# Linear attention with a gated FFN on one core: reciprocals spread to the head rows by DMA, contractions padded to 128 rows, weights folded and read in another order

## The chip, the cores and the metric

The kernel runs on one core of a Trainium2 chip. The metric is the device time of one execution in microseconds (us). It is 310.28 us for the kernel before, the median of three runs between 310.15 and 311.46. One slow run of the kernel before took 315.74 us at a granted clock of 0.978, the six fast ones beside it 309.21 to 312.18 us at 0.988 to 1.0.

Engines are named as in the profile: PE is TensorE (PEld its weight loads), DVE is VectorE, ACT is ScalarE, POOL is GpSimd, and SP is SyncE, which issues most DMAs.

## The reference

One block of 2,048 tokens, width 640, 32 heads of 20 columns, then a gated FFN of width 1,536. All inputs are bfloat16.

```python
phi(y) = concat(softmax(y), softmax(-y))           # per head, 40 features
q, k, v = split(layernorm(x) @ wqkv)
pq, pk  = phi(q @ w_phi), phi(k @ w_phi)           # w_phi: one 20x20 matrix per head
kv, z   = pk^T v, sum_tokens(pk)                   # per head, over ALL tokens
h  = x + ((pq kv) / (pq z + 1e-6)) @ wo
h2 = h + ((layernorm(h) @ w_gate) * (layernorm(h) @ w_up)) @ w_down
```

Because `kv` sums over all tokens, the kernel has a KV stage (all sixteen 128-token tiles of k and v), then a transition (first numerators, first output projections), then an FFN stage into which the remaining q work is mixed.

## The kernel before: the parts that matter here

The kernel records its instructions as units and puts them into a fixed tuned order (a list `ORDER`). `cost`, `lat` and `dma` are only what the scheduler was told; they don't run on the chip.

The heads are cut into six chunks: five of six heads (120 rows) and one of two heads (40 rows). In a chunk's PSUM tile, rows 0 to 5 (or 0 and 1) hold the denominators and the numerators start at row 6 (`HG`). A reciprocal must be multiplied into the 20 rows of its head. Before, a small matmul with a 0/1 matrix `Em` copied each reciprocal to its 20 rows:

```python
def num_mm(b, c, pr):                      # contraction over kr = 120 or 80 rows
    mm(pr[0:m, 0:n], KV[0:kr, c, 0:m],      q[0:kr, c, :], True, False)
    mm(pr[0:m, 0:n], KV[0:kr, NG + c, 0:m], q[0:kr, NG + c, :], False, True)
    ...                                    # cut: the last chunk has one matmul

def expand(b, c, pr, m, em, rden):
    n = P * BLK[b][1]                      # 256 or 512 tokens
    mm(pr[0:m, 512:512 + n], em, rden, True, True)      # contraction over 6 or 2 rows
    rx = rx_p.new()
    ...                                    # cut: PSUM -> rx copy on ACT or DVE
    tt("vector", oT[b][0:m, n * c:n * (c + 1)], pr[0:m, 0:n], o, ALU.mult)

def num(b):
    for c in range(6):
        ...                                # num_mm, then
        act(lnd[0:nh, 0:n], pr[0:nh, 0:n], ACT.Ln)      # 1/d = exp(-ln d)
        act(rden[0:nh, 0:n], lnd[0:nh, 0:n], ACT.Exp, scale=-1.0)
        expand(b, c, pr, m, Em[0:nh, 0, 0:m], rden[0:nh, 0:n])

def watt(t):                               # output projection of one tile
    for c in range(6):
        m = HG + DH * (HG if c < NG else 2)             # 126 or 46 rows
        for (n0, n1) in ((0, 512), (512, D)):
            mm(pr[:, n0:n1], oT[b][0:m, ...], Wo6[0:m, c, n0:n1], c == 0, c == 5)
```

The softmax here doesn't subtract the row's maximum and nothing guards it: scores larger than these inputs give would overflow.

Of the kernel before, what the change touches and what calls it, by code (L numbers as in the profile page):

```python
# [495 lines left out]
6 0 16 7 1 11 12 24 2 17 19 13 30 43 49 39 45 51 5 8 3 14 27 10 4 15 18 9 29 32 21 25 22 34 37 42 56 58 61 66 69 73 47 52 36 40 44 48 38 46 50 53 20  # L496
23 26 28 31 33 35 41 71 77 64 70 68 74 59 65 55 62 57 63 72 54 60 67 75 79 82 86 98 85 89 95 106 87 101 109 121 139 142 198 218 78 88 92 80 84 91 94
100 103 108 111 110 117 76 83 81 90 96 115 126 131 199 221 123 135 119 124 132 145 185 193 223 224 97 102 105 93 99 107 113 116 125 128 134 129 138
112 120 104 114 118 133 140 153 230 227 149 144 127 160 154 173 184 169 175 147 155 189 196 177 187 141 148 136 146 152 161 201 208 232 228 122 170
179 183 157 168 182 194 200 204 206 219 207 211 192 202 130 137 143 150 176 180 249 275 181 191 151 158 164 214 234 239 292 303 159 197 205 174 195  # L500
213 215 217 229 235 241 240 254 156 166 163 172 178 188 210 222 333 307 278 291 250 261 265 272 284 288 334 308 162 237 257 262 226 260 264 269 273
279 282 286 283 294 236 243 242 252 258 268 295 300 335 331 267 276 259 270 277 287 313 317 381 389 244 251 297 255 263 281 299 304 312 316 321 315
328 293 311 271 280 289 323 338 340 384 393 374 375 377 379 380 399 400 403 404 406 414 416 318 327 309 322 325 339 348 352 385 397 419 356 363 324
332 349 344 351 359 391 398 421 336 343 342 347 337 354 360 371 395 401 422 362 368 346 353 355 365 370 390 409 408 423 165 186 171 301 310 248 314
190 167 290 245 274 306 326 364 345 369 203 212 216 220 231 238 247 253 266 209 225 233 246 256 298 319 329 341 412 415 410 413 427 429 430 433 434
437 441 378 387 382 392 426 402 425 432 436 443 450 463 445 442 444 449 466 464 469 474 448 447 457 461 453 452 458 462 470 468 472 477 478 479 483
489 494 504 508 510 517 518 525 530 505 514 520 524 538 536 543 546 285 296 302 305 320 330 358 418 439 350 357 361 366 372 373 388 405 420 471 482
486 484 488 496 481 490 493 500 487 491 495 497 503 501 506 507 499 498 502 519 529 531 535 537 512 511 516 522 547 561 572 576 582 580 590 593 539
549 571 573 578 585 592 596 367 376 383 386 394 396 407 438 455 411 417 424 428 435 440 451 459 475 431 446 454 460 465 480 526 533 544 456 467 473
476 485 492 509 515 527 581 599 601 597 604 605 554 560 564 559 563 568 575 583 587 619 623 624 567 577 586 591 600 602 613 617 618 562 570 574 584  # L510
595 598 627 632 633 631 638 640 644 647 635 645 654 661 667 670 676 680 607 611 612 675 684 686 603 608 609 622 626 629 610 614 615 625 628 630 634
636 637 663 668 669 674 679 682 687 692 694 700 704 707 643 646 648 653 656 658 639 641 642 649 651 652 681 685 688 695 697 699 709 716 724 727 732
733 741 747 719 728 736 738 755 743 748 754 729 737 742 745 750 751 760 769 715 721 726 731 739 758 762 764 521 550 553 557 558 579 589 594 606 513
523 528 532 540 542 551 556 565 534 541 545 548 552 555 566 569 588 766 774 775 777 780 782 787 789 793 616 620 621 683 690 693 666 672 677 740 749
752 659 664 671 722 730 734 735 753 757 761 767 696 702 759 768 772 807 813 814 797 801 802 794 798 799 800 804 805 803 806 810 812 816 817 847 850
855 858 862 865 824 827 830 833 836 838 808 809 811 818 821 823 831 835 840 848 852 854 829 832 837 841 844 846 849 853 857 859 863 867 869 874 876
877 880 881 885 891 868 870 871 872 875 887 893 904 878 886 890 892 896 897 915 917 873 879 882 883 888 901 905 916 650 655 657 660 662 665 673 678
691 706 710 712 713 717 718 723 725 744 689 698 701 703 705 708 711 714 720 746 756 763 765 770 771 776 778 786 790 795 796 815 820 822 773 781 783
819 825 828 779 784 788 785 791 792 842 851 856 860 864 866 889 899 903 908 826 834 839 843 845 861 894 902 910 913 924 928 929 933 937 938 936 941
943 918 922 923 940 946 947 927 931 932 884 895 900 907 911 914 958 962 964 967 969 972 898 906 912 939 942 944 948 952 954 957 960 966 968 971 974  # L520
979 982 983 973 977 980 984 986 987 996 1002 1004 1005 1008 1009 1016 1020 989 993 994 995 998 1013 1017 1021 1001 1007 1011 1012 1014 1018 1025 1030
992 997 999 1000 1003 1023 1028 1031 909 919 920 951 949 956 945 950 953 930 934 935 921 925 926 955 959 963 961 965 970 976 978 975 985 988 990 991
981 1015 1022 1029 1032 1006 1010 1019 1024 1027 1054 1058 1059 1033 1037 1038 1036 1040 1041 1045 1049 1050 1060 1064 1065 1066 1068 1069 1039 1043
1044 1057 1061 1062 1026 1034 1035 1051 1055 1056 1042 1046 1047 1048 1052 1053 1070 1073 1076 1080 1082 1067 1078 1081 1084 1085 1063 1072 1083 1086
1087 1071 1074 1075 1077 1079
# [10 lines left out]
def _build(ctx, nc, A_x, A_wqkv, A_w_phi, A_wo, B_w_gate, B_w_up, B_w_down, out):  # L536
# [19 lines left out]
    o0 = NT * 2 * D - 4 * NC * D - NC * 160  # L556
    Wnat, WT = [], []
    for w in range(2):
        Wnat.append(r1[:, o0:o0 + NC * D].rearrange("p (c n) -> p c n", c=NC))
        WT.append(r1[:, o0 + NC * D:o0 + 2 * NC * D].rearrange("p (a n) -> p a n", a=NC))  # L560
        o0 += 2 * NC * D
# [11 lines left out]
    rx_p = pool("rx", r2, 7168, 512, 2)  # L573
    ot_p = pool("ot", r2, 8192, D, 3)
# [22 lines left out]
    Em = view(sb("Em", 4 * P), "p (j n) -> p j n", j=4)  # L597
# [55 lines left out]
    def copy(eng, o, i):  # L653
        n = numel(o)
        if eng == "any":
            return R.add("vector", lambda e: e.tensor_copy(real(o), real(i)), [i], [o], cost=(n + 130) / 960.0,  # L656
                         alts=[("scalar", lambda e: e.activation(out=real(o), in_=real(i), func=ACT.Copy), 0.17 + n / 1200.0)])
        if eng == "scalar":
            return act(o, i, ACT.Copy)
        return R.add(eng, lambda e: e.tensor_copy(real(o), real(i)), [i], [o], cost=(numel(o) + 130) / 960.0)  # L660
# [10 lines left out]
    def load_x(t0, n):  # L671
        return dma(x_all[:, t0:t0 + n, :], A_x[0, P * t0:P * (t0 + n), :].rearrange("(t p) n -> p t n", p=P), n * 163840, reads=[], eng="scalar")
# [3 lines left out]

    load_x(0, 1)
    load_x(1, 1)
    R.add("scalar", lambda e: e.preload_act_table_set("natural_log_exp_and_others"), cost=1.3)
    dma(Wrows, A_w_phi.rearrange("h d f -> (h d) f").rearrange("(a p) f -> p a f", p=P), 25600, reads=[])  # L680
    load_w(Wnat[0], D)
    load_w(Wkv[:, :, D:2 * D], 2 * D)
    load_x(2, 2)
    load_x(4, 4)


    memset("gpsimd", Gm[:, :, :], 1.0)
    memset("gpsimd", ident[:, :], 0.0)
    afsel(ident[:, :], ALU.not_equal, 1.0, 0, [[-1, P]], 1)
    afsel(Gm[:, :, :], ALU.is_ge, 0.0, 0, [[P, NC], [-DH, H]], 1)  # L690
    afsel(Gm[:, :, :], ALU.is_ge, 0.0, DH - 1, [[-P, NC], [DH, H]], -1)
    for a in range(NC):
        lo, hi = CH[a]
        nh = hi - lo + 1
        tt("gpsimd", Phi[:, a, 0:nh, :], Wrows[:, a, :].unsqueeze(1).to_broadcast([P, nh, DH]),
           Gm[:, a, lo:hi + 1].unsqueeze(2).to_broadcast([P, nh, DH]), ALU.mult)
# [5 lines left out]
    memset("gpsimd", Zd[:, :, :], 1.0)  # L702
    memset("gpsimd", G6[:, :], 1.0)
    memset("gpsimd", Em[:, :, :], 1.0)
# [7 lines left out]
    afsel(Em[:, :, :], ALU.is_ge, 0.0, -HG, [[32 * DH, 4], [1, P]], -DH)  # L712
    afsel(Em[:, :, :], ALU.is_ge, 0.0, HG + DH - 1, [[-32 * DH, 4], [-1, P]], DH)
# [15 lines left out]
    def ln_apply(t, dst):  # L729
# [5 lines left out]
                                                         scalar2=mv[:, t, 3:4], op0=ALU.subtract, op1=ALU.mult), 0.7)])  # L735
# [3 lines left out]
    def fold_T(w, a):  # L739
        pb = psum.new(1)  # L740
        tb = pb.bitcast(BF16)
        with R.group():
            for a2 in range(NC):
                o, i = tb[:, P * a2:P * (a2 + 1)], Wnat[w][:, a2, P * a:P * (a + 1)]
                R.add("tensor", lambda e, o=o, i=i: e.transpose(out=real(o), in_=i, identity=ident[:, :]),  # L745
                      [i, ident[:, :]], [o], cost=0.1, lat=0.17)
        copy("any", WT[w][:, a, :], tb[:, 0:D])
# [271 lines left out]
    for a in range(NC):  # L1019
        fold_T(0, a)  # L1020
# [104 lines left out]
```

## Time and profile before

| | kernel before |
|---|---|
| time, median of 3 | 310.28 us |
| profiled execution (slow) | 316.35 us, span 314.6 us, mean granted clock 0.978 |
| PE busy | 298.4 us, 95% of the span |
| first denominator matmul (end of the KV stage) | 82.7 us |
| first gate/up matmul (start of the FFN stage) | 110.4 us, after 10.2 us at half clock |

These lines are from the summary page of the kernel before: the span, PE's busy time and share, PE's busy share and granted clock in 40 slices (a digit is tenths), and the chain of work that ended last, by engine.

```profile
span 314.6 us, 5099 instructions
...
PE 298.4 (95%) x2024; PEld 165.3 (53%) x2024; DVE 178.2 (57%) x321; ACT 158.2 (50%) x345; POOL 82.5 (26%) x58
...
PE   2899599999989999999999999999999999999995
...
PEclk9999899999957999999999999999999999999999
...
PE 77%; DMA 9%; POOL 6%; DVE 4%; ACT 1%; SPq 1%; issue 0%
```

PE is the limit: its row stands at 9 in nearly every slice, and 77% of the chain is PE. The 5 and 7 in the clock row are the 10.2 us at half clock. The timed runs of the same kernel had a granted clock of 0.994 to 1.0, so that stretch belongs to the slow profile and not to the 310 us.

The next lines are groups of matmuls of the kernel before, one line per shape. The columns are: line, engine, operation, output tile <- input tiles, rows*columns of the weights, rows x columns of the moving operand, count | busy us, mean ns of one | idle time before them.

```profile
L628 PE MATMUL ps<-wo,r 126*128 126x128 bf16 x80 | 17.8, 223 | 0.0
...
L628 PE MATMUL ps<-rden,Em 6*126 6x512 bf16 x15 | 6.4, 425 | 0.0
...
L628 PE MATMUL ps<-wo,r 46*128 46x128 bf16 x16 | 3.5, 216 | 0.0
L628 PE MATMUL ps<-rden,Em 6*126 6x256 bf16 x10 | 3.3, 378 | 0.0
```

These mean times are from start to modelled end, and neighbours overlap, so they can't be added. For a busy PE, the distance from one matmul's start to the next one's start is what counts, and I worked that out from the trace: 0.356 us for the 6-row, 512-column expansion, where a 128-row matmul of 512 columns takes 0.216; and 0.148 us for the 128-column matmul of the 46-row chunk, and about the same (0.152) for the 126-row one just before it, where others take 0.056.

### The profile page before, as it was taken

How to read it: one execution, taken by the hardware profiler on the slowest of the kernel's cores; microseconds unless marked ns; L12 is line 12 of the kernel's file. 1: busy time of each engine (PE TensorE's matmuls, PEld its weight loads, DVE VectorE, ACT ScalarE, POOL GpSimd, SP SyncE). 2: the span in 40 equal slices, each digit the busy share in tenths (PEclk: the TensorE clock that was granted, in tenths of full speed). 3: DMA queues.
4: the chain of work that ended last, by engine and by line, in shares of the span. 5: the costliest groups of instructions: out<-in, count | busy, mean ns of one | idle time of the engine just before them, and what ended most of it. 6: DMA issues, size and time to landing. Idle time of an engine off the chain costs nothing.

```text
span 314.6 us, 5099 instructions
## 1 busy us (share of the span) xinstructions
PE 298.4 (95%) x2024; PEld 165.3 (53%) x2024; DVE 178.2 (57%) x321; ACT 158.2 (50%) x345; POOL 82.5 (26%) x58
## 2 busy tenths in 40 slices
PE   2899599999989999999999999999999999999995
PEld 2555375657634588656465444445444444544453
DVE  4979669787846794365867324544434445423204
ACT  4779488866354854358276233638423443532200
POOL 6217854879931463003332300000000000000000
PEclk9999899999957999999999999999999999999999
DMA  7767929994960666002074500004100002300002
GB/s 237 206 96 163 234 69 189 217 190 136 260 133 2 133 70 113 2 21 58 11 141 78 93 0 2 22 23 85 42 2 0 0 21 65 83 2 0 0 2 83
DMA packets 58171, 25.84 MB, mean 82 GB/s; under 512 B 49279, under 2 KB 56867, under 8 KB 58147
## 3 DMA queue, kind: packets, MB, share of 16 engines
q1 hardware_dynamic: 56003, 22.89, 34.1%
q10 hardware_dynamic: 2144, 2.62, 3.0%
q8 instruction: 16, 0.26, 0.3%
q14 instruction: 8, 0.07, 0.1%
HBM read 11.05 MB, written 2.62 MB: 43 GB/s over the span
## 4 chain that ended last, share of the span: by engine, by line
PE 77%; DMA 9%; POOL 6%; DVE 4%; ACT 1%; SPq 1%; issue 0%
PE ps L628 77%; POOL r L645 4%; DMA r<-in_A_wqkv_dram 4%; DMA xnT<-xn 3%; DVE sr L768 2%; DMA pqT<-phq 2%; POOL phq L645 2%; PE ps L745 1%; SPq L622 1%; DVE sr L770 1%; ACT phq L639 0%; DVE st L718 0%; DVE xn L734 0%; DVE r L1003 0%; DVE wkv L656 0%
## 5 line engine op out<-in xcount | busy, mean ns | idle before, releaser
L628 PE MATMUL ps<-xnT,wgu 128*128 128x512 bf16 (+1 forms) x600 | 106.6, 337 | 0.0
L639 ACT ACTIVATE r<-ps 128x640 bf16<-128x640 f32 (+2 forms) x108 | 62.8, 595 | 73.8 <-PE ps L628 73.1
L645 DVE TENSOR_TENSOR r<-ps,r 128x512 bf16<-128x512 f32 (+5 forms) x90 | 51.5, 581 | 63.2 <-PE ps L628 51.8
L628 PEld LDWEIGHTS ps<-xnT,wgu 128*128 128x128 bf16 x600 | 57.8, 98 | 46.3 <-issue 1.7
L628 PE MATMUL ps<-r 128*128 128x512 bf16 (+5 forms) x620 | 72.8, 269 | 3.8 <-DMA r<-in_A_wqkv_dram 3.4
L628 PEld LDWEIGHTS ps<-r 128*128 128x128 bf16 (+2 forms) x620 | 44.0, 108 | 31.3 <-DMA r<-in_A_wqkv_dram 3.6
L645 POOL TENSOR_TENSOR phq<-phq,sr 128x1320 bf16<-128x1320 bf16 x16 | 38.7, 2424 | 63.3 <-DVE sr L806 61.3
L628 PE MATMUL ps<-wkv,xnT 128*128 128x512 bf16 x320 | 47.1, 305 | 2.0 <-DMA xnT<-xn 2.0
L645 POOL TENSOR_TENSOR r<-r,sr 128x1280 bf16<-128x1280 bf16 x16 | 37.5, 2362 | 27.1 <-DVE sr L770 23.8
L628 PEld LDWEIGHTS ps<-wkv,xnT 128*128 128x128 bf16 x320 | 24.9, 99 | 21.0 <-issue 3.4
L639 ACT ACTIVATE phq<-ps 128x600 bf16<-128x600 f32 (+1 forms) x64 | 24.7, 436 | 16.8 <-PE ps L628 14.7
L628 PE MATMUL ps<-wo,r 126*128 126x512 bf16 x192 | 30.8, 307 | 0.0
L1003 DVE SCALAR_TENSOR_TENSOR r<-ps,mv,x_all 128x640 bf16<-128x640 f32 x16 | 14.1, 883 | 23.8 <-PE ps L628 23.8
L628 PE MATMUL ps<-wq,xnT 128*128 128x512 bf16 (+1 forms) x160 | 25.3, 309 | 1.2 <-ACT lnd L639 1.2
L804 DVE TENSOR_REDUCE sr<-phq 128x66 f32<-128x1320 bf16 x16 | 24.2, 1512 | 3.0 <-ACT phq L639 2.2
L768 DVE TENSOR_REDUCE sr<-r 128x64 f32<-128x1280 bf16 x16 | 23.4, 1470 | 3.6 <-ACT r L639 2.2
L628 PEld LDWEIGHTS ps<-wo,r 126*128 126x128 bf16 x192 | 14.1, 99 | 15.5 <-issue 7.7
L964 DVE SCALAR_TENSOR_TENSOR x_all<-ps,x_all 128x640 bf16<-128x640 f32 x16 | 13.2, 823 | 11.7 <-PE ps L628 11.5
L628 PEld LDWEIGHTS ps<-wq,xnT 128*128 128x128 bf16 x160 | 12.5, 100 | 11.3 <-ACT lnd L639 1.6
L639 ACT ACTIVATE lnd<-ps 6x512 f32<-6x512 f32 (+3 forms) x22 | 11.9, 547 | 11.6 <-PE ps L628 11.3
L914 DVE CAST r<-ps 126x512 bf16<-126x512 f32 (+2 forms) x14 | 8.6, 615 | 15.4 <-PE ps L628 15.3
L968 ACT ACTIVATE xn<-x_all,mv 128x640 bf16<-128x640 bf16 x9 | 7.4, 827 | 17.3 <-DVE mv L650 17.3
(57 smaller groups left out, 171.2 us busy)
## 6 DMA issues: line engine op xcount, KB each, us to landing
out_dram<-r SPq DMA_DIRECT2D x16, 160.0 KB, 1.8
x_all<-in_A_x_dram ACTq DMA_DIRECT2D x3, 640.0 KB, 6.5
wgu<-in_B_w_up_dram SPq DMA_DIRECT2D x5, 384.0 KB, 3.9
wgu<-in_B_w_gate_dram SPq DMA_DIRECT2D x5, 384.0 KB, 4.3
r<-in_B_w_down_dram SPq DMA_DIRECT2D x6, 320.0 KB, 6.3
r<-in_A_wqkv_dram SPq DMA_DIRECT2D x1, 800.0 KB, 5.0
wkv<-in_A_wqkv_dram SPq DMA_DIRECT2D x1, 800.0 KB, 10.0
wo<-in_A_wo_dram SPq DMA_DIRECT2D x4, 157.5 KB
```

The lines of the kernel that those rows point to most:

```text
L622: return R.add("sync", lambda e: e.dma_start_transpose(real(dst), real(src)), rd, wr, cost=1.03 + 0.17 * nbytes / 163840, lat=1.0, dma=0.3 ...
L628: return R.add("tensor", lambda e: e.matmul(real(o), lhsT=real(l), rhs=real(r), start=start, stop=stop, **kw), [l, r], [o], cost=cost or m ...
L639: return e.activation(out=real(o), in_=real(i), func=func, scale=scale, **kw)
L645: return R.add(eng, lambda e: e.tensor_tensor(out=real(o), in0=real(a), in1=real(b), op=op), [a, b], [o], cost=cost)
L745: R.add("tensor", lambda e, o=o, i=i: e.transpose(out=real(o), in_=i, identity=ident[:, :]), [i, ident[:, :]], [o], cost=0.1, lat=0.17)
L768: R.add("vector", lambda e: e.tensor_reduce(out=real(sr)[:, 0:n], in_=real(v), axis=AX.X, op=ALU.add), [v], [sr[:, 0:n]], cost=0.13 + n * ...
L770: R.add("vector", lambda e: e.reciprocal(out=real(sr)[:, 66:66 + n], in_=real(sr)[:, 0:n]), [sr[:, 0:n]], [sr[:, 66:66 + n]], cost=0.56)
L804: R.add("vector", lambda e: e.tensor_reduce(out=real(r4(0)), in_=real(k4), axis=AX.X, op=ALU.add), [k4], [r4(0)], cost=0.13 + n * DH / 960.0)
L914: lat=0.08, alts=[("vector", lambda e: e.tensor_copy(real(o), real(i)), (n + 130) / 960)])
L964: R.add("vector", lambda e: e.scalar_tensor_tensor(out=h, in0=real(pr)[:, 0:D], scalar=1.0, in1=h, op0=ALU.mult, op1=ALU.add, accum_out=sm ...
L968: R.add("scalar", lambda e: e.activation(out=real(k), in_=h, func=ACT.Identity, bias=nm), [h, nm], [k], cost=0.83, lat=0.08, alts=[("vecto ...
L1003: R.add("vector", lambda e: e.scalar_tensor_tensor(out=real(k), in0=real(pr)[:, 0:D], scalar=r2, in1=h, op0=ALU.mult, op1=ALU.add), [pr[:, ...
```

## The change

The change does five things at once:

1. The `Em` matmul and its PSUM copy go. A DMA on SP's queue reads each of the 6 (or 2) rows of reciprocals and writes it to the 20 rows of its head in an SBUF buffer `rx` (four buffers).
2. The contractions of numerator and output projection are padded to 128 rows, so that PE has no row-count changes there. POOL clears `KV`, `rx` and the output weights `Wo6` for that, early.
3. Wk is loaded in five row pieces, and each piece is transposed as it lands.
4. The FFN's gate and up weights are read in the second half of the KV stage, x is loaded two tiles at a time, and some costs told to the scheduler were corrected.
5. The tuned order is a new one (the whole list of more than 1,000 numbers differs).

```diff
-    def expand(b, c, pr, m, em, rden):
-        n = P * BLK[b][1]
-        mm(pr[0:m, 512:512 + n], em, rden, True, True)
         rx = rx_p.new()
-        ...  PSUM -> rx copy on ACT or DVE
-        tt("vector", oT[b][0:m, n * c:n * (c + 1)], pr[0:m, 0:n], o, ALU.mult)
+        dst, o = rx[HG:HG + DH * nh, 0:n], oT[b][:, n * c:n * (c + 1)]
+        def spread(e):
+            v = real(rden)
+            (ps, k), inner = v.ap
+            return e.dma_start(real(dst), bass.AP(v.tensor, v.offset, [[ps, k], [0, DH], list(inner)]))
+        R.after(rx_clear, R.add("sync", spread, [rden], [dst], cost=0.45, lat=1.6, dma=0.25 + 0.0006 * n))
+        tt("vector", o, pr[:, 0:n], rx[:, 0:n], ALU.mult)
 ...
-                mm(pr[0:m, 0:n], KV[0:kr, c, 0:m], q[0:kr, c, :], True, False)
-                mm(pr[0:m, 0:n], KV[0:kr, NG + c, 0:m], q[0:kr, NG + c, :], False, True)
+                mm(pr[:, 0:n], KV[:, k, :], q[:, k, :], k == ks[0], k == ks[-1])
 ...
-                    mm(pr[:, n0:n1], oT[b][0:m, n * c + q:n * c + q + P], Wo6[0:m, c, n0:n1], c == 0, c == 5)
+                    mm(pr[:, n0:n1], oT[b][:, n * c + q:n * c + q + P], Wo6[:, c, n0:n1], c == 0, c == 5)
 ...
+    kv_clear = memset("gpsimd", KV[:, :, :], 0.0)
+    rx_clear = memset("gpsimd", rx_r[:, :], 0.0)
+    wo_clear = memset("gpsimd", Wo6[:, :, :], 0.0)
 ...
-    load_w(Wnat[0], D)                       # Wk in one 800 KB load
+    for i in range(1, NC):
+        first(load_k(i))                     # Wk in five row pieces
 ...
-            bulk(6 + 2 * c + g, Wgu[:, g, c, :], ...)     # behind KV tile 6 to 15
+            bulk(9 + c, Wgu[:, g, c, :], ...)             # behind KV tile 9 to 13
```

The expression `[[ps, k], [0, DH], ...]` is the spread's source: k rows (6 or 2), each read 20 times.

## The prediction

> **What bounds the kernel now.** TensorE. The summary has PE busy 95% of a 314.6 us span, DVE 57%, ACT 50%, POOL 26%; the chain of waits gives PE 77%, one unbroken piece from 88.1 to 311.4 us. Start-to-start times of neighbouring matmuls in the trace sum to 305 us; at their own best rate (0.216 us for 512 columns, 0.056 for 128) the same columns need about 278. The other 27 us are waits (first matmul at 5.96 us behind the 800 KB key-weight load; 3.4 us at 33 us for the transposed Wq; 0.4 to 1.6 us a few more times), half clock for 3.4 and 10.2 us, and matmuls that cost more than their columns. The profiled run is a slow one (316.4 us against 310.3); I take its 10.2 us at half clock to be most of that.
>
> **What the change removes.**
> 1. 30 reciprocal-expanding matmuls with 6 or 2 rows, 9.5 us of PE by start-to-start. A 6-row, 512-column one costs 0.356 us, not 0.216[...].
> 2. [...] its 128-column matmul takes 0.148 instead of 0.056, and so does the one ahead of it, 16 times each: 3 us. Around the numerator matmuls 1 to 1.5 us. Padding to 128 rows removes these and adds no columns.
> Both are on the critical path, as PE hardly waits after 88 us: 13 to 14 us.
> 3. 30 PSUM copies of the expanded reciprocals (13 us on ACT and DVE): off the path.
> 4. Front: Wk by row pieces starts the transposes about 2 us earlier, but all 25 still precede the folds. Gain about 2 us.
> 5. FFN weights later, x in two-tile loads, Wq transposes scheduled with a higher cost: the 3.4 us wait for Wq and the half clock after it mostly go: 2 to 4 us.
>
> **What it adds.** 30 spreading DMAs (about 0.45 us of issue each, from the plain DMAs' issue times). From denominator to scaled numerator the expand and copy (about 1.3 us) become an estimated 2.5 us (1.8 us landing of a 160 KB store in the DMA list, plus waiting behind transposes). In the FFN blocks other matmuls fill this. In the two small blocks between KV stage and FFN they do not: 18 numerator matmuls are followed directly by the output projection, with four spread buffers for twelve chunks, and ScalarE's Ln stands behind q exponentials that wait for transposes. I expect 2 to 4 us of PE idle there. POOL's 7 us of extra clearing (estimate from 0.53 us per 512 columns) falls where it idles, 10 to 22 us.
>
> **Sum.** 310.3 - 13.5 - 2 - 3 + 3 = about 295.0 us, range 289.0 to 302.0. Chances: faster 0.92, within 2% 0.06, slower 0.02.
>
> **What the profile should show.** No 6-row matmuls; the 128-column output-projection matmul at 0.056 throughout; PE busy down by about 13 us, ACT by about 8; first matmul at 3.5 to 4.5 us; no wait over 1.5 us for Wq; a new PE wait on DVE's products or the spreads near 85 to 95 us; PE unbroken in the FFN stage.
>
> **What would make it wrong.** Spreads that land later than 3 us and stall the output projection in every block (300 or more); a transition idle long enough to halve the clock for 10 us; or the old profile's half clock being in its timed runs too, and vanishing (288).

The extra time of matmuls at a change of row count was measured (0.356 us where a 128-row matmul takes 0.216, 0.148 where others take 0.056). Item 2 is about the 46-row chunk of the output projection.

## More of the kernel before

Busy time by stage (KV stage, transition, FFN stage) in the kernel before: stretch, its length, then busy time and instructions of each engine, granted clock, DMA share and GB/s.

```profile
0.00:82.70 82.70, 70.96 (x645) 45.99 (x649) 63.34 (x118) 57.50 (x110) 52.38 (x46) 0.98 0.77 182
82.70:110.40 27.70, 26.48 (x156) 12.27 (x154) 18.07 (x40) 16.20 (x48) 11.12 (x6) 0.82 0.57 100
110.40:314.60 204.20, 201.00 (x1231) 107.08 (x1229) 96.75 (x164) 84.49 (x188) 19.05 (x8) 1.00 0.19 39
```

In the FFN stage PE is busy for 201.0 of 204.2 us. The KV stage is the only one where it waits noticeably.

## The result

The changed kernel is correct and slower. Its median is 333.67 us (four runs, 333.06 to 335.6, all fast) against 310.79 us for the kernel before in the same rounds. The ratio is 1.0747, with a 95% interval from 1.0692 to 1.0801. A ratio here and below is the mean time of one kernel's fast runs over the mean of the other's fast runs of the same rounds, so it is not quite the ratio of the medians quoted beside it.

The same lines of the summary page, for the kernel after (a fast run):

```profile
span 333.7 us, 5044 instructions
...
PE 290.8 (87%) x1994; PEld 166.7 (50%) x1994; DVE 175.4 (53%) x309; ACT 149.5 (45%) x328; POOL 87.4 (26%) x58
...
PE   2798899898773886998899997999999959999995
...
PEclk9999799999795899799999998999999998999999
...
PE 51%; DMA 15%; DVE 14%; POOL 7%; SPq 6%; issue 4%; ACT 2%; DVEq 0%; ACTq 0%
```

PE lost about 8 us of busy time, as hoped, but the span grew by 19 us. The chain of waits, which was 77% PE, is now 51% PE and 15% DMA, 14% DVE. PE has holes (7, 7, 3, 5 in its row). The clock row drops around the longer ones: stretches at half clock follow the holes of 3.4, 2.1 and 2.7 us at 131, 204 and 272 us. Holes of 1.2 to 1.6 us at 117, 155 and 160 us have none behind them.

The same three stages in the kernel after. Its first denominator matmul starts at 91.6 us and its first gate/up matmul at 122.4 us.

```profile
0.00:91.60 91.60, 75.23 (x651) 49.28 (x651) 72.29 (x121) 58.37 (x112) 61.44 (x48) 0.96 0.71 175
91.60:122.40 30.80, 20.32 (x140) 10.16 (x138) 17.86 (x39) 12.73 (x40) 10.13 (x5) 0.83 0.64 92
122.40:333.70 211.30, 195.29 (x1209) 107.26 (x1207) 85.23 (x150) 78.37 (x180) 15.79 (x7) 0.97 0.25 45
```

All three stages are longer: by 8.9, 3.1 and 7.1 us. (Against a fast run of before the transition's difference is larger: 10.2 us at half clock in the profile before can cost up to 5.1, an estimate: a 512-column matmul takes 0.426 us from start to start at half clock there, 0.216 at full.) In the transition PE is idle for 10.5 of 30.8 us, in the FFN stage for 16.0 of 211.3.

The extra time is gone. These are the output projection's groups in the kernel after:

```profile
L626 PE MATMUL ps<-wo,r 128*128 128x512 bf16 x96 | 30.3, 412 | 6.9 <-DVE r L643 6.9
L626 PE MATMUL ps<-wo,r 128*128 128x128 bf16 x96 | 22.2, 231 | 2.7 <-DVE r L643 2.7
```

One shape is left, and its start-to-start time at the median is 0.056 us for 128 columns in the trace. But a new entry stands behind the last bar: 9.6 us of waiting for DVE's products, where before it said 0.0. What those products wait for is shown by everything that touches the buffer `rx` in the kernel after: the 30 spreads (their time is the issue on SP), the 30 products, what the products waited for, and who waited for the products.

```profile
L923 SPq DMA_DIRECT2D rx<-rden x30: 677/758/1740, 93.0 to 266.0; - x30
L643 DVE TENSOR_TENSOR r<-ps,rx x30: 415/691/693, 96.8 to 273.6; 128x512 bf16<-128x512 f32 x18, 128x256 bf16<-128x256 f32 x12
...
  DMA rx<-rden: 54.9, 25
...
  PEld ps L626: 21.1, 11
  PE ps L626: 17.4, 11
```

25 of 30 products had to wait for their spread, 54.9 us in all, and PE in its turn waited 17.4 us for products, 11 times. From the start of a spread's issue to the start of its product the trace gives 5.16 us at the median, 3.24 at the least, 7.60 at the most.

The longest one, in the last block, in the chain of waits of the kernel after (start, length, what):

```profile
254.84 8.67 PE ps L626 x49
...
265.02 0.61 ACT rden L637
265.64 0.32 ACT r L637
265.95 7.57 DMA rx<-rden
...
273.55 0.70 DVE r L643
274.25 0.05 issue
274.30 10.81 PE ps L626 x66
```

A spread of 7.6 us stands between ACT and DVE, and the chain comes back to PE only after it. PE had other work meanwhile, but one matmul starts at 271.25 us and the next one only 3.05 us later, 2.66 of it idle. Before, this part of the chain was inside one unbroken piece of PE, 223 us long:

```profile
88.11 223.30 PE ps L628 x1351
```

What one spread does was read from its packets. One that ran alone (issued at 240.79 us) shows 120 packets of 1,024 bytes and six small packets of 4 bytes. The first packet starts 1.43 us after the start of the issue and the last data packet ends at 4.74 us. The six small packets are completion writes. I take each for one DMA engine, so six engines: at most six of the 120 packets are in flight at once. In what was measured the number of these writes goes with the source's rows: two for the two-row spread issued at 260.06 us, six here, 12 in a_twelve (12 rows), 15 in a_wide (120 rows). The transfer took 3.3 us for 120 KB, 20 rows per engine. Two of the engines started a row every 0.08 us and had ended by 3.05 us after the start of the issue; the other four took about 0.17 us a row and ended the transfer.

The front did not gain. These are PE's first instructions in the kernel after:

```profile
4.00 0.69 PE L753 MATMUL ps<-ident,r 128*128 128x128 bf16 x5 [4.00 <-DMA r<-in_A_wqkv_dram]
7.28 2.31 PE L753 MATMUL ps<-ident,r 128*128 128x128 bf16 x20 [2.59 <-DMA r<-in_A_wqkv_dram]
```

Transposes begin at 4.0 us instead of 5.96, and then wait 2.6 us for the second Wk piece. The first projection of the KV stage starts at 12.2 us (12.3 before).

And on DVE the second layer norm of the front stands out (start, length, instruction), beside POOL's clearing of the output weights:

```profile
11.77 3.01 DVE L742 TENSOR_SCALAR xn<-x_all,mv 128x640 bf16<-128x640 bf16 x1
...
15.61 0.45 DVE L742 TENSOR_SCALAR xn<-x_all,mv 128x640 bf16<-128x640 bf16 x1
```

```profile
8.35 1.27 POOL L661 MEMSET KV<- 128x1408 bf16 x1
9.56 1.80 POOL L661 MEMSET rx<- 128x2048 bf16 x1
11.30 3.30 POOL L661 MEMSET wo<- 128x3840 bf16 x1
```

The same instruction takes 0.45 us at 15.6 us and 3.01 us at 11.8 us, ending just after POOL's memset (14.78 and 14.60 us). Not every DVE instruction beside a memset was slow: a copy from PSUM at 10.85 us took 0.82 us, as long as one at 15.97 us, after the memsets. That POOL held the layer norm off is my reading of the times; a_split and a_late test it. The second k/v projection starts at 17.4 us, 2.4 later than before.

### The profile page after: what moved, and what is told of

It reads as the page before. It is cut to its first block, busy times and chain, and to the rows that moved or that the text cites. A ratio compares the mean times of both kernels' runs of the same rounds, so it can differ in the third digit from the quotient of the medians.

```text
span 333.7 us, 5044 instructions
## 1 busy us (share of the span) xinstructions
PE 290.8 (87%) x1994; PEld 166.7 (50%) x1994; DVE 175.4 (53%) x309; ACT 149.5 (45%) x328; POOL 87.4 (26%) x58
## 4 chain that ended last, share of the span: by engine, by line
PE 51%; DMA 15%; DVE 14%; POOL 7%; SPq 6%; issue 4%; ACT 2%; DVEq 0%; ACTq 0%
PE ps L626 50%; DMA rx<-rden 12%; POOL r L643 6%; SPq L620 4%; DVE sr L778 4%; DVE sr L814 3%; SPq L923 2%; DMA r<-in_A_wqkv_dram 2%; POOL phq L643 1%; DVE r L643 1%; DMA x_all<-in_A_x_dram 1%; DVE sr L816 1%; DVE sr L780 1%; ACT r L637 1%; PE ps L753 1%
## 5 line engine op out<-in xcount | busy, mean ns | idle before, releaser
L626 PE MATMUL ps<-xnT,wgu 128*128 128x512 bf16 (+1 forms) x600 | 110.3, 341 | 3.4 <-DVE r L643 3.4
L626 PEld LDWEIGHTS ps<-xnT,wgu 128*128 128x128 bf16 x600 | 58.8, 99 | 51.3 <-DVE r L643 4.1
L637 ACT ACTIVATE r<-ps 128x512 bf16<-128x512 f32 (+2 forms) x92 | 52.0, 574 | 66.1 <-PE ps L626 60.4
L626 PE MATMUL ps<-r 128*128 128x512 bf16 (+5 forms) x620 | 74.3, 276 | 6.4 <-POOL r L643 3.2
L626 PEld LDWEIGHTS ps<-r 128*128 128x128 bf16 (+2 forms) x620 | 47.5, 113 | 32.4 <-POOL r L643 3.8
L643 DVE TENSOR_TENSOR r<-ps,r 128x512 bf16<-128x512 f32 (+1 forms) x60 | 34.1, 577 | 50.3 <-PE ps L626 43.4
L643 DVE TENSOR_TENSOR r<-ps,rx 128x512 bf16<-128x512 f32 (+1 forms) x30 | 17.4, 584 | 55.0 <-DMA rx<-rden 54.9
L626 PE MATMUL ps<-wo,r 128*128 128x512 bf16 x192 | 30.8, 321 | 9.6 <-DVE r L643 9.6
L626 PEld LDWEIGHTS ps<-wkv,xnT 128*128 128x128 bf16 x320 | 24.6, 98 | 22.1 <-DVE wkv L654 2.1
L626 PE MATMUL ps<-wq,xnT 128*128 128x512 bf16 (+1 forms) x160 | 26.3, 314 | 4.1 <-DVE r L643 4.1
L626 PEld LDWEIGHTS ps<-wo,r 128*128 128x128 bf16 x192 | 15.9, 105 | 23.7 <-DVE r L643 11.0
L976 ACT ACTIVATE xn<-x_all,mv 128x640 bf16<-128x640 bf16 x9 | 7.2, 825 | 27.3 <-DVE mv L648 25.3
```

The costliest lines, as they stand in the source:

```text
L626: return R.add("tensor", lambda e: e.matmul(real(o), lhsT=real(l), rhs=real(r), start=start, stop=stop, **kw), [l, r], [o], cost=cost or m ...
L637: return e.activation(out=real(o), in_=real(i), func=func, scale=scale, **kw)
L643: return R.add(eng, lambda e: e.tensor_tensor(out=real(o), in0=real(a), in1=real(b), op=op), [a, b], [o], cost=cost)
L976: R.add("scalar", lambda e: e.activation(out=real(k), in_=h, func=ACT.Identity, bias=nm), [h, nm], [k], cost=0.83, lat=0.08, alts=[("vecto ...
```

## The experiments

My theory after the result had two parts. **W**: the spreads take about twice the time that the order was made for, and that makes the transition and the FFN stage longer. **P**: POOL's early clearings hold DVE off and make the KV stage longer. Rivals were the new order as such, the traffic of the spreads on SP's queue, the later FFN weight loads, and the padding itself being worth less than thought.

Kernels named a_ are built from the kernel after, those named b_ from the kernel before. Four of the a_ kernels give a wrong result. The quoted expectations were written call by call; where one names theories by letters of its own, the words beside the letter count.

This table gathers the stage boundaries of the profiled runs; it is worked out from the first denominator matmul and the first gate/up matmul in each trace. "PE clock halved" lists the lengths of the stretches at half clock before the last matmul.

| kernel | KV stage | transition | FFN stage | PE clock halved, us | median us |
|---|---|---|---|---|---|
| before (slow run) | 82.7 | 27.7 | 204.2 | 3.4, 10.2 | 310.79 |
| after | 91.6 | 30.7 | 211.3 | 3.4, 3.4, 10.2, 3.4, 3.4, 3.4 | 333.67 |
| a_free | 89.2 | 31.1 | 192.4 | 10.2 | 315.20 |
| a_twelve | 92.7 | 24.9 | 194.0 | 3.4, 3.4, 3.4 | 311.75 |
| a_wide | 89.8 | 25.3 | 193.0 | 3.4, 6.8 | 310.26 |
| a_split | 92.6 | 30.4 | 210.9 | 3.4, 3.4, 10.2, 3.4, 3.4, 3.4 | 335.91 |
| a_late | 86.6 | 31.3 | 210.4 | 13.7, 3.4, 3.4 | 331.29 |
| a_latev | 88.7 | 30.0 | 211.5 | 3.4, 10.2, 3.4, 3.4, 3.4 | 331.53 |
| a_wlate | 87.2 | 24.6 | 193.0 | 3.4 | 306.65 |
| b_pad2 | 82.3 | 20.9 | 197.7 | 3.4 | 303.23 |
| b_padk2 | 82.3 | 22.5 | 200.6 | 3.4 | 306.77 |
| b_padw | 83.4 | 23.9 | 197.0 | 3.4, 3.4 | 307.81 |

The medians are over all runs; those of a_wlate and b_padw hold slow ones (306.25 and 306.40 without them). b_pad, a_expand, a_list and a_slow are left out and told below. Rows of the same order can be compared stage by stage: the eight from after to a_wlate, and the b_ rows with before. The two orders place the q work differently, so across them only the totals compare. The rows are single profiles, and they scatter: after, a_free, a_twelve and a_wide do nearly the same work up to the first spread, and yet their KV stages end between 89.2 and 92.7 us.

### a_free: nobody waits for a spread (wrong result)

The spreads write to a spare place, and the products read a constant. The order is that of the kernel after.

```diff
-        R.after(rx_clear, R.add("sync", spread, [rden], [dst], ...))
-        tt("vector", o, pr[:, 0:n], rx[:, 0:n], ALU.mult)
+        # scheduled as before, but written to a spare buffer and never read
+        u = R.add("sync", spread_to_spare, [rden], [dst], ...)
+        # the product reads rows of ones
+        u = R.add("vector", product_with_ones, ...)
```

> The kernel after, every instruction in the same order, but the spreads go to a spare buffer and the products read a constant, so nobody waits for a spread (wrong result on purpose). Theory L (latency of the spreads is what TensorE waits for after 92 us): the waits for products and spreads after 92 us, about 26 us, and most of the half clock after them go, 300 to 308 us. Rival K (the loss is in the KV stage and its new order): over 325 us. Either way the first denominator matmul stays at about 91 us.

Measured: 315.2 us median (four fast runs), ratio to before 1.0145, interval 1.0083 to 1.0206. The waits for spreads are gone, and the FFN stage falls from 211.3 to 192.4 us. The transition doesn't improve: spreads now go out without the products' throttle and pile up in the queue, a q transpose issued behind them holds PE for 9.7 us at 104.7 us, and 10.2 us at half clock follow. So the run says that the FFN stage's loss is the waits for spreads. For the transition it is spoilt by a wait of its own making. a_wide was the cleaner test.

### a_wide: the same waits, a copy that 15 engines carry (wrong result)

The spread copies 120 rows from a constant tile of 120 rows instead of 6 rows twenty times. It has the same bytes, the same issue and the same waits, and still waits for the reciprocals. POOL has one more memset early, for the constant.

```diff
-            return e.dma_start(real(dst), bass.AP(v.tensor, v.offset, [[ps, k], [0, DH], list(inner)]))
-        R.after(rx_clear, R.add("sync", spread, [rden], [dst], ...))
+            return e.dma_start(real(dst), wsrc[HG:HG + DH * nh, 0:n])
+        R.after(rx_clear, R.add("sync", spread, [rden, wsrc[:, 0:n]], [dst], ...))
```

> The kernel after in the same order, same waits, same bytes, but each spread copies 120 rows from a 120-row source instead of 6 rows read 20 times (wrong result on purpose). Theory L1 (the six source rows confine the copy to six DMA engines, 20 rows one after another on each): the wait from issue to product falls from about 5.1 us to under 3 us, and the time by more than half of what a_free gains, 310 to 320 us. Rival L2 (issue time and place in the sync queue behind transposes make the latency): still over 4.5 us per spread and over 328 us.

Measured: 310.26 us median, ratio 0.9976, interval 0.99 to 1.0053. That is 23 us less than the kernel after, with nothing but the copy's source and that memset changed. What touches `rx` in a_wide:

```profile
L922 SPq DMA_DIRECT2D rx<-wsrc x30: 733/810/1520, 92.1 to 246.3; - x30
...
  DMA rx<-wsrc: 12.7, 13
...
  PEld ps L627: 7.1, 5
  PE ps L627: 5.5, 4
```

The issue on SP is as long as before (0.81 us at the median; 0.76 in the kernel after), so the issue isn't the cause. The products' waits fall from 54.9 to 12.7 us, PE's waits for them from 17.4 to 5.5. From issue to product it takes 2.57 us at the median. A quiet copy shows 15 completion writes and 0.61 us of transfer. The transition loses 5.4 us and the FFN stage 18.3; 1.8 us of the difference lie in the KV stage, before any spread, and are within the scatter. W is confirmed for the loss against the kernel before: the order is good for 310 us if a spread takes 2.6 us. What makes the spread slow isn't settled by this run alone, as the copy has both more engines and other source rows.

### a_twelve: a dose in between (wrong result)

Each spread reads a constant of 12 rows, each row ten times. I expected 12 engines to carry it.

```diff
-            return e.dma_start(real(dst), wsrc[HG:HG + DH * nh, 0:n])
+            v = wsrc[0:2 * nh, 0:n]
+            (ps, k), inner = v.ap
+            return e.dma_start(real(dst), bass.AP(v.tensor, v.offset, [[ps, k], [0, DH // 2], list(inner)]))
```

> The changed kernel in its own order, with each spread copying a constant of 12 rows, every row to 10 rows (wrong result on purpose; same bytes, same waits). Theory (an engine writes its rows one after the other, so a spread's time goes by rows per engine: 20 with six engines, 10 with twelve, 8 with fifteen): 12 completion writes, issue to product about 3.4 us at the median (between 5.2 with six engines and 2.6 with fifteen), and a total of 314 to 321 us. Rival (rows repeated from one source row are slow in themselves, whatever the number of engines): issue to product 4.5 us or more, total above 326. Second rival (only the number of engines counts below some size): as the 120-row copy, 310 to 312.

Measured: 311.75 us median, ratio 0.9997, interval 0.9917 to 1.0078. A quiet spread shows 12 completion writes and 1.72 us of transfer (1.87 in a second one); from issue to product it takes 3.63 us at the median. So the latency is near what the theory said (about 3.4), and the first rival falls as far as it says that the number of engines doesn't count. But the total, 311.75, is below the theory's 314 to 321; it is that of the second rival. The lines of `rx` in a_twelve say why:

```profile
L924 SPq DMA_DIRECT2D rx<-wsrc x30: 672/798/1322, 94.1 to 249.1; - x30
...
  DMA rx<-wsrc: 30.0, 20
...
  PEld ps L627: 7.6, 7
  PE ps L627: 5.5, 6
```

DVE's products wait 30.0 us for the spreads, more than twice as long as in a_wide, yet PE waits for the products no longer than there, 5.5 us. The order has room for a spread of 3.6 us. It has none for 5.2. The loss is not proportional to the latency. It sets in between the two.

The transfer times also tell how the rows cost. Ten rows per engine took 1.72 us and twenty took 3.32, both about 0.17 us for a row of the engine that ends last. Eight different rows per engine took 0.61 us, 0.08 a row. It isn't enough that the same source row is read again and again: two of the six engines in the kernel after read so at 0.08 us a row, and so did both of its two-row spread at 260.06 us (20 rows each, 1.6 us). What makes a row cost 0.17 us isn't shown. So a_wide gained twice: fewer rows per engine, and cheaper rows. How much each is worth can be estimated from these figures: six engines with 20 rows each at 0.08 us would transfer in about 1.5 us, 0.9 more than a_wide, and take about 3.5 us from issue to product, no longer than a_twelve, which lost nothing. By this estimate six engines alone would not have cost the 23 us; it took the dear rows too. A run with six engines and 120 different source rows would separate the two. There is none, so this stays open.

### a_split: clearings in small pieces

If POOL's memset holds DVE off for the length of an instruction, short memsets should let DVE in between.

```diff
-    wo_clear = memset("gpsimd", Wo6[:, :, :], 0.0)
+    wo_clear = pieces(Wo6[:, :, :])          # memsets of 256 columns; KV and rx too
```

> The kernel after in the same order, but POOL's three clears (6.4 us in three instructions) are cut into pieces of 256 columns. Theory P (VectorE's bf16 scale op at 11.8 us takes 3.0 instead of 0.4 us because a POOL clear holds it off): that op is under 0.8 us, the second KV projection starts about 2 us earlier, total 1 to 3 us less. Rival: the op is slow for another reason, no change.

Measured: 335.91 us median, ratio 1.0794, interval 1.0733 to 1.0855. It gained nothing. DVE and then POOL in the trace of a_split:

```profile
11.46 4.46 DVE L752 TENSOR_SCALAR xn<-x_all,mv 128x640 bf16<-128x640 bf16 x1
```

```profile
9.85 2.09 POOL L674 MEMSET rx<- 128x256 bf16 x8
11.87 3.86 POOL L674 MEMSET wo<- 128x256 bf16 x15
```

The DVE instruction now lasts 4.46 us, until POOL's last piece has ended at 15.73, and not until the end of the piece that was running. Memsets that followed one another without a gap held this instruction off here (4.46 us) as one long one did (3.01 us). By what means isn't shown; what the runs show is the coincidence in time, and 0.45 us again once the memsets are elsewhere (a_late, below).

### a_late and a_latev: clearings later

a_late moves the clearings behind POOL's second normalisation, and writes them as 4-byte words, which takes half the time (0.95 us for `rx`, 1.80 before). a_latev also puts two copies of v back on ACT that the change had let go to DVE.

```diff
+    kv_clear, rx_clear, wo_clear = cleared(KV), cleared(rx_r), cleared(Wo6)   # 4-byte words
+    # in the finished order they are moved behind POOL's second normalisation
```

> The kernel after, every order kept, but POOL's three clears are written as 4-byte words and moved behind POOL's second normalisation, where VectorE has no bf16 scale op. a_split showed that the clears hold VectorE off until POOL falls idle. If that delay at 12 to 17 us carries through the KV stage: the bf16 scale op near 11.8 us takes under 0.5 us, the second KV projection starts at 15.0 to 15.5 instead of 17.4 us, and the first denominator matmul comes 1.5 to 2.5 us earlier than 91.6 us; total about 331 us. If the KV stage makes it up later: denominator within 0.7 us of 91.6.

> a_late, and the two value copies that the kernel after put on VectorE go back to ScalarE, where the kernel before has all sixteen. If VectorE's load at the end of the KV stage makes TensorE wait (1.7 us at 85 us for such a copy): first denominator matmul another 1 to 2 us earlier than in a_late. If the normalisation chain on POOL sets the end of the stage: no earlier than in a_late.

Measured: a_late 331.29 us (ratio 1.0675, interval 1.0606 to 1.0744), a_latev 331.53 us (1.0646, 1.058 to 1.0711). In a_late the layer norm takes 0.45 us again, the second k/v projection starts at 14.5 us (17.4 in the kernel after) and the KV stage ends at 86.6 us, 5.0 earlier. So P is confirmed at the front. The 5.0 us are not all its own: the kernel after has 6.8 us at half clock in its KV stage and a_late has none. Against a_free, which has none there either and the early clearings, a_late is 2.6 us earlier. The totals are 2.4 us below the kernel after's, and the intervals overlap, so a gain at the end isn't clear of noise here; in a_late 13.7 us at half clock follow at 94.9 us. In a_latev the KV stage ends no earlier (88.7), so the place of the v copies isn't what is left of its delay.

### a_wlate: both causes taken away (wrong result)

```diff
 a_late, with the 120-row copy of a_wide
```

> The changed kernel in its own order, with the 120-row copies of a_wide (wrong result on purpose) and the late clearings of a_late. If the two causes simply add: first denominator matmul at about 86.6 us and a total about 5 us below a_wide's 310.3, so 304 to 306.5. If the gain of the late clearings is lost to waits on POOL's normalisation and on the clock rather than to the spreads: 308 to 310.5, no faster than a_wide.

Measured: 306.65 us median, ratio 0.9838, interval 0.9769 to 0.9908 (one of the four runs was slow and is left out of the ratio). Against a_wide's ratio of 0.9976 that is 1.4% or about 4.3 us, nearly the 5 us of the first theory; the two intervals just touch. The first denominator matmul came at 87.2 us (86.6 expected), 2.6 us before a_wide's. So the clearings' gain reaches the end when spreads don't hold the kernel up afterwards, and W and P add up as far as these few runs can show it.

### b_pad and b_pad2: the padding alone, in the old kernel

These keep the `Em` matmul and the old order, and pad all contractions to 128 rows, those of `Em` too. b_pad clears in small pieces early, b_pad2 in 4-byte words, with the clearings of `Wo6` and of the reciprocal buffers behind POOL's third normalisation. Both are correct. Both also drop one small load of output weights (7.5 KB), which the cleared rows make needless.

```diff
-            mm(pr[0:m, 0:n], KV[0:kr, c, 0:m], q[0:kr, c, :], True, False)
+            mm(pr[0:m, 0:n], KV[0:128, c, 0:m], q[0:128, c, :], True, False)   # m = 128
 ...
-            expand(b, c, pr, m, Em[0:nh, 0, 0:m], rden[0:nh, 0:n])
+            expand(b, c, pr, m, Em[:, 0, :], rden[:, 0:n])
```

> The kernel before, its order and its expanding matmuls kept, but every contraction of numerator, expansion and output projection padded to 128 rows and 128 columns (clears cut into small pieces). [...] 6-row expansion 0.216 instead of 0.356 us, 128-column output projection 0.056 throughout, 8 us less, about 302 us. If the row count does not matter: 310 us.

> b_pad with the clears written as 4-byte words (half the elements) and placed where VectorE has no bf16 scale op: KV's ahead of the Phi products, Wo's and the denominators' after the third normalisation. If the 3.9 us wait at 11.8 us in b_pad came from a clear holding VectorE off: that wait goes, 3 us less, 302 to 303 us. If not: 305 to 306 us.

b_pad's first figures are for the case that the extra time goes with the changes of row count.

Measured: b_pad 305.6 us (ratio 0.9834, interval 0.9778 to 0.9889), with a PE wait of 3.9 us at 11.8 us that the early clearings cause. b_pad2 303.23 us (six runs, 302.34 to 306.08; ratio 0.972, interval 0.9656 to 0.9783), without that wait. b_pad2 beats both kernels. Its matmul groups:

```profile
L642 PE MATMUL ps<-wo,r 128*128 128x128 bf16 x96 | 21.0, 219 | 0.0
...
L642 PE MATMUL ps<-rden,Em 128*128 128x512 bf16 x18 | 6.7, 379 | 0.0
```

The expansion takes 128 rows now: its mean time has fallen from 425 ns to 379, and from start to start it takes 0.216 us instead of 0.356.

### b_padk2: which padding pays

b_pad2 with the expansions back at 6 and 2 contraction rows.

```diff
-            expand(b, c, pr, m, Em[:, 0, :], rden[:, 0:n])
+            expand(b, c, pr, m, Em[0:nh, 0, :], rden[0:nh, 0:n])
```

> b_pad2 (0.972 of the kernel before), but the expanding matmuls are back at 6 and 2 rows, the rest stays padded. By start-to-start in the kernel before, a 6-row expansion costs 0.14 us over a full one[...]: 30 x 0.2 = 6 us of the gain belong to it, so about 0.99 of the kernel before. [...]

The 0.2 us are the 0.14 us and about 0.1 us more at the matmul before each expansion (in the kernel before, 0.148 us for 128 columns there instead of 0.056). The rival was that the extra time belongs to the output projection alone: 0.972 to 0.976.

Measured: 306.77 us (six runs), ratio 0.9879, interval 0.9831 to 0.9927. Its expansions:

```profile
L642 PE MATMUL ps<-rden,Em 6*128 6x512 bf16 x15 | 5.8, 384 | 0.0
```

Against b_pad2 (0.972, on another chip and with other runs of the kernel before) the expansions' row changes cost 1.6% or about 5 us. Padding numerators and output projection is worth the remaining 1.2%, about 3.8 us. Not all of that is rows: b_padk2 keeps the 128 weight columns, and with them a 6-row expansion takes 0.317 us from start to start, where with 126 columns it took 0.356. So of the 0.14 us over a full matmul, 0.10 belong to the rows and 0.04 went with the columns.

### b_padw: the later FFN weight loads

b_pad2 with the ten gate and up loads moved behind KV tiles 9 to 13.

```diff
             u = bulk(6 + 2 * c + g, Wgu[:, g, c, :], ...)
+            u.ops[0].late = kv_u[9 + c][0].ops[-1]        # moved behind KV tile 9 + c
```

> b_pad2 with one part of the change added: the ten FFN weight loads are issued from KV tile 9 on as in the kernel after, all compute orders kept. If the loads' traffic makes the wait for the transposed Wq (2.9 us at 33 us) and the half clock after it: that wait under 1.5 us and 2 to 4 us less than b_pad2, 0.960 to 0.966 of the kernel before. If not: 0.970 to 0.975.

Measured: 307.81 us median over six runs, two of them slow (306.40 without these); ratio of the fast ones 0.9868, interval 0.9808 to 0.9928, so 1.5% worse than b_pad2 (on another chip), which neither expectation had. PE's wait for the transposed Wq is 3.0 us at 32.9 us from start to start, as long as in b_pad2 (2.9). So early FFN weights are not what delays Wq, and reading them later gains nothing here. The kernel after has these later loads too; no run shows what they cost in its order.

### a_expand, a_list, a_slow: is it the order?

a_expand is the kernel after with the padded `Em` matmul in place of the spreads. a_list is the kernel after without its fixed order, scheduled by the kernel's own list scheduler. a_slow is a_list with the scheduler told what a spread really takes.

```diff
 a_slow against a_list
-        R.add("sync", spread, [rden], [dst], cost=0.45, lat=1.6, dma=0.25 + 0.0006 * n)
+        R.add("sync", spread, [rden], [dst], cost=0.75, lat=3.6, dma=0.8)
```

> The kernel after with its loads, front and ORDER, but the spreads given back to TensorE as expanding matmuls padded to 128 rows plus a PSUM copy (correct result; the schedule moves somewhat because each chunk has one unit more). If the spread is the whole loss and the KV stage's new loads and order are neutral: 300 to 304 us, below the kernel before. If the KV stage of the kernel after is itself slower by about 8 us, as its first denominator matmul at 91.6 against 82.7 us says: 308 to 314 us.

> Control: the kernel after with the fixed ORDER taken out, so that its own list scheduler orders everything with the unchanged costs (spread 0.45 us issue, about 2.2 us to land). Its time is only there for a_slow to be compared with; 330 to 345 us.

> As a_list, but the scheduler is told what the trace shows of a spread: 0.75 us of issue, about 5 us to landing. If the loss is that the order was made for a 2.2 us latency (theory O): waits for products after 92 us shrink by half or more, 10 us or more below a_list. If a 5 us latency cannot be hidden with two denominator buffers and four spread buffers (theory B): within 4 us of a_list.

Measured: a_expand 332.55 us (ratio 1.065, interval 1.0582 to 1.0718). That is outside both expectations, and it decides nothing. One unit more per chunk moved the whole schedule: its first denominator matmul came at 104 us. So the old order of units can't be kept while a unit is added, and the run mixes two changes. a_list 368.18 us (1.1768, 1.1683 to 1.1853; 330 to 345 expected) and a_slow 360.88 us (1.1542, 1.1468 to 1.1617). Knowing the true latency brings the plain scheduler 7.3 us, between what the two theories expected. Both are far above the tuned order's 333.67, so a plain schedule is not a fair test of what a tuned one could do. Whether a tuning that knew 5.2 us could hide it stays open.

## Why the prediction was wrong

The prediction said 295.0 us, 289.0 to 302.0, and 0.92 for faster by over 2%. The kernel takes 333.67 us.

- **The step that failed** is "From denominator to scaled numerator the expand and copy (about 1.3 us) become an estimated 2.5 us". From issue to product alone it is 5.16 us. I took the 2.5 us from a 160 KB store's landing of 1.8 us, without asking how many engines carry the spread. The six-row source got six engines here (six completion writes), with 20 rows each: 3.3 us of transfer. With a copy that 15 engines carry and that reads 120 different rows, a_wide measured 2.57 us, and the 23 us were gone. So my latency was right for a kind of copy that the kernel does not make. The outcome itself was on the prediction's list of what would make it wrong: "Spreads that land later than 3 us and stall the output projection in every block (300 or more)".
- **"In the FFN blocks other matmuls fill this"** rested on the first number. It would have held at 2.5 us, and it still held at 3.6 (a_twelve: FFN stage 194.0 us). At 5.2 us it did not: 211.3 against 193.0. The new order had been made with 0.45 us of issue and about 1.6 us plus 0.25 and 0.0006 per column of landing, and by a_twelve and the kernel after it has room for 1 us more than that, but not for 2.6.
- **"I expect 2 to 4 us of PE idle" in the transition** named the right place with too small a size: PE is idle there for 10.5 us, against 1.2 before. With the fast copies of a_wide it is about 5, and the stage is 5.4 us shorter.
- **The clock** was named in "a transition idle long enough to halve the clock for 10 us". It came: 10.2 us at 100.7 us, and five stretches of 3.4 us elsewhere, 27.2 us together, against 10.2 in a_wide. At half clock a 512-column matmul takes 0.427 us from start to start instead of 0.216, so a busy PE loses half the time; this is at most 8.5 of the 23 us, an estimate from those lengths. How long a hole it takes was not shown: the stretch at 206.5 us follows a hole of 2.05 us, while one of 1.8 us at 13.8 us has none behind it.
- **"POOL's 7 us of extra clearing ... falls where it idles"** was wrong in its consequence. POOL did idle there, and the clearings take 6.4 us. But DVE's layer norm stood still meanwhile, and the KV stage got 2.6 to 5.0 us longer (a_late against a_free and the kernel after). At the end that was about 4.3 us without the slow spreads (a_wlate); with them the 2.4 us of a_late are not clear of noise.
- **Front, "Gain about 2 us"**: PE began 2 us earlier and then waited 2.6 us for the second Wk piece. The first k/v projection started 0.1 us earlier. Gain: none.
- **"the 3.4 us wait for Wq and the half clock after it mostly go"** was half right. PE no longer waits for Wq's DMA between 28 and 40 us of the kernel after; the fourth of Wq's five transposes, which ended the wait before, lands at 31.3 us instead of 36.4. But four other waits came in its place at 32 to 38 us, two that a copy on ACT ends and two that a normalisation on POOL ends: 2.6 us idle against 3.4, and 3.4 us at half clock come with them, as before. So the gain was about 0.9 us. b_padw shows that the later weight loads alone don't remove the wait for Wq; whether the x loads or the new order did stays open.
- **The extra time at changes of row count** was there to be saved. The 46-row matmul's 0.148 us became 0.056, and b_pad2, which keeps the expansions, is 2.8% faster than before (8.7 us). A part of the 0.14 us that I put down to the rows went with the 126 weight columns (b_padk2). The mechanism that I named for it was not shown.
- **The other signs**: PE busy went down by 8 us (13 predicted; the half clock is in both figures), ACT by 8.7 (8 predicted). PE was not unbroken in the FFN stage.

What accounts for the 23 us more: the kernel after with fast copies and late clearings (a_wlate, wrong result) is 1.6% faster than before. The clearings take back 1.4% of that, and the slow spreads cost the 23 us on top. So even without both causes only about 5 of the 15 us forecast are there: the front gained nothing, Wq about 0.9 us, and the KV stage is still 4.5 us longer (87.2 against 82.7). What stays open: 2.5 to 4.6 us of the KV stage's delay (86.6 us in a_late and 88.7 in a_latev against 82.7; I put 1.4 us down to one q tile more that the new order starts there), which of the two makes a spread slow, the engines or the rows, and whether another order could hide a 5 us spread.

## What to carry to other kernels

Before a broadcast by DMA replaces a matmul, count the engines and look at what each reads: here a source with six outer rows put six engines to work on twenty rows each, four of them at 0.17 us a row where a copy of different rows took 0.08, and 0.36 us of PE plus a copy became 5.2 us of latency. This order, tuned for one latency, hid a longer one (3.6 us) for nothing and lost 23 us at 5.2, with the halved clock on top, so ask what the slack is before trusting that "other matmuls fill it". And the cheap half of a change can be the good one: padding contractions to a single row count, with the clearings placed where DVE has no instruction that they hold off, gave 2.8% without any of the rest.
